# Cutting sixteen weight rows into transfers of 5, 5, 5 and 1 instead of four of 4

## The chip, the core and the metric

The kernel runs on one core of one Trainium2 chip. The metric is the device time of one execution in microseconds. A core has five engines with instruction streams of their own: PE (matrix multiply), DVE (vector), ACT (scalar), POOL and SP. SP does no arithmetic here; it issues the transfers from the chip's main memory into the core's working memory, which has 128 rows ("partitions"). The transfers themselves are carried by 16 DMA engines.

## The reference

Two identical rounds, each an attention block over a long cache for one new token and then a gated feed-forward block, in float32, for two sequences:

```python
B, Sq, D = 2, 1, 512
Hq, Hkv, Sk, Dh = 32, 8, 32768, 128
...
q = (x @ wq).reshape(B, Sq, Hq, Dh).transpose(0, 2, 1, 3)
k = jnp.repeat(k_cache, Hq // Hkv, axis=1)
v = jnp.repeat(v_cache, Hq // Hkv, axis=1)
p = softmax(einsum("bhqd,bhkd->bhqk", q, k) * Dh ** -0.5)
o = einsum("bhqk,bhkd->bhqd", p, v)
A(x) = o.transpose(0, 2, 1, 3).reshape(B, Sq, Hq * Dh) @ wo
B(x) = (gelu(x @ w_gate) * (x @ w_up)) @ w_down        # 512 -> 1792 -> 512
...
x = x + A(layernorm(x)); x = x + B(layernorm(x))
x = x + A(layernorm(x)); x = x + B(layernorm(x))
```

The two caches are read in full in both rounds: over a gigabyte of float32 in all, for little arithmetic on each byte.

## The kernel before

The work is a stream. All inputs are listed once, at the start, in the order in which they will be used (`add`, lines 246 to 275): for each of the two layers the query weights, then for each of the 16 pairs of a cache head and a sequence its keys and values, with the output weights of a head between the halves of its values, and last the feed-forward weights. Layer 1 walks the pairs backwards, so that it begins with what layer 0 has still in memory.

One large tile, `mem`, of 110 units of 512 float32 in each of 128 partitions, takes everything. A full cache piece is 32 units: 64 KB in each of 128 partitions, 8.4 MB. `pump` (line 193) takes the next entry of the stream, looks for a free place in `mem`, and issues its transfer on the SP queue; when there is no place it stops, and is called again whenever `done` gives a place back. So three cache pieces circulate, and SP issues a transfer as soon as the matmuls that read the old content have ended. Transfers of one queue are carried in the order of their issue.

For each pair, `scores` multiplies the keys (L443), `softmax` follows on DVE and ACT, `values` multiplies the values (L512), and `combine` and `project` multiply the result by the head's output weights into the accumulator W.

Nearly all transfers fill 128 partitions. For two heads, listed in `NARROW`, a part of the output weights is laid out otherwise: 2 of 4 query heads' weights of cache head 6 in layer 0, and 3 of 4 of cache head 1 in layer 1. They lie in 16 partitions (`NROW`) as 8 groups (`NSEL`) per query head. A row holds 8 x 512 float32 for each query head: 32 KB in layer 0, 48 KB in layer 1. `narrow` (line 532) uses them: it spreads the result over 16 rows (L538) and multiplies group by group (L546). The remaining query heads' weights come by an ordinary 128-partition transfer issued right behind, and are used in L556.

The sixteen rows are fetched by four transfers, number i taking rows i, i + 4, i + 8 and i + 12. The host arranges `won` so that these four lie together. All four go out one after another on the SP queue (L209) as soon as there is room, and `narrow` waits for all of them.

Of the kernel before, what the change touches and what calls it, by code (L numbers as in the profile page):

```python
# [18 lines left out]
HKV = 8  # L19
REP = 4  # L20
DM = 512
# [42 lines left out]

NARROW = {(0, HKV - 2): 2, (1, 1): 3}
NROW = 16
NSEL = P // NROW


def pieces(split):  # L70

    out, s = [], 0
    for n in split:
        out.append((s, n))
        s += n
    return out


def parts(kind, l, pair):

    if kind == "k":
        return K_PARTS[l].get(pair, pieces(PLAIN))
    return pieces(V_SPLIT[l].get(pair, PLAIN))
# [59 lines left out]
def block_kernel(ctx: ExitStack, tc: tile.TileContext, x, consts, kt, vt, wq, wo, won, gu, wd, out):  # L143
    nc = tc.nc
# [5 lines left out]
    mem = cp.tile([P, UNITS * UNIT], F32, name="mem")  # L150
# [6 lines left out]
    def take(key, n):  # L157
        if key in planned:
            o = planned[key]
            if not any(s <= o and o + n <= e for s, e in holes):  # L160
                return None
        elif n == CHUNK:
            spots = [o for o in range(0, UNITS - CHUNK + 1, CHUNK)
                     if any(s <= o and o + n <= e for s, e in holes)]
            if not spots:
                return None
            o = spots[0]
        else:
            fit = [(e - s, -s, e) for s, e in holes if e - s >= n]
            if not fit:  # L170
                return None
            size, s, e = min(fit)
            o = -s
        for i, (s, e) in enumerate(holes):
            if s <= o and o + n <= e:
                holes[i:i + 1] = [(x, y) for x, y in ((s, o), (o + n, e)) if y > x]
                return o
        return None
# [14 lines left out]
    def pump():  # L193
        while stream:
            key, src, rows, cols = stream[0]
            n = CHUNK if rows == NROW else cols / UNIT if key in planned else -(-cols // UNIT)
            o = take(key, n)
            if o is None:
                return
            stream.popleft()  # L200
            if key == LAST_ROOM:
                held.append(ROOM[1])
            c = int(o * UNIT)
            at[key] = (o, n), mem[:rows, c:c + cols]
            if rows == NROW:


                for i in range(4):
                    nc.sync.dma_start(mem[i:NROW:4, c:c + cols], src[i])  # L209
            else:  # L210
                nc.sync.dma_start(at[key][1], src)

    def flat_of(key):
        if key not in at:
            pump()
        return at[key][1]

    def get(key, a):
        return flat_of(key).rearrange("p (a c) -> p a c", a=int(a))

    def done(key, s=0, n=None):

        o, size = at[key][0]
        n = size if n is None else n
        if s + n == size:
            del at[key]
        give(o + s, n)
        pump()
# [3 lines left out]
    def flat(src, g, b, s, n):  # L232
        h, c = divmod(s, CHUNK)
        return src[b, g, h, :, c * UNIT:(c + n) * UNIT]

    def add(key, src, rows, cols):
        stream.append((key, src, rows, cols))

    def meets(l, n):

        return (l == 0 and n == len(ORDER) - 1), (l == 1 and n == 0)

    def wo_group(l, g):
        return next(t for t in WO_GROUPS[l] if g in t)

    for l in range(2):
        for i, (s, m) in enumerate(pieces(WQ_SPLIT[l])):
            add(("wq", l, i), wq[:, s * DM:(s + m) * DM], P, m * DM)
        for n, (g, b) in enumerate(orders[l]):
            second = meets(l, n)[1]  # L250
            vp = parts("v", l, (g, b))
            for s, m in parts("k", l, (g, b)):
                add(("k", l, g, b, s), flat(kt, g, b, s, m), P, m * UNIT)
            for s, m in [] if second else vp:
                if n % 2 == 1 and s == vp[1][0] and not meets(l, n)[0]:
                    group = wo_group(l, g)
                    o = g % 2 * HALF
                    if (l, g) in NARROW:
                        h = NARROW[l, g]
                        add(("won", l, g), won[l, :, :, :h * NSEL * DM], NROW, h * NSEL * DM)  # L260
                        add(("wo", l, g), wo[g // 2, :, o + h * DM:o + HALF], P, (REP - h) * DM)
                    elif len(group) == 2 and g == group[0]:
                        add(("wo", l, g), wo[g // 2], P, 2 * HALF)
                    elif len(group) == 1:
                        add(("wo", l, g), wo[g // 2, :, o:o + HALF], P, HALF)
                add(("v", l, g, b, s), flat(vt, g, b, s, m), P, m * UNIT)
            if meets(l, n)[0]:

                add(("wo", l, g), wo[g // 2, :, g % 2 * HALF:(g % 2 + 1) * HALF], P, HALF)
        for e in range(2):  # L270
            half_of = gu[e * P * FH:(e + 1) * P * FH].rearrange("(p c) -> p c", p=P)
            for j, (c, m) in enumerate(pieces(GU_SPLIT[l][e])):
                add(("gu", l, KC * e + j), half_of[:, c:c + m], P, m)
        for j, (o, m) in enumerate(pieces(WD_SPLIT[l])):
            add(("wd", l, j), wd[:, o * DM:(o + m) * DM], P, m * DM)
# [15 lines left out]
    nc.scalar.dma_start(xT, x)  # L291
    nc.scalar.dma_start(cst, consts)
    pump()
    ident = cst[:, C_ID:C_ID + P]

# [44 lines left out]
    def big():  # L340

        state["turn"] = 1 - state["turn"]
        if state["alone"] or state["turn"]:
            return big_desk[:, :]
        return mem[:, held[0] * UNIT:(held[0] + 1) * UNIT]
# [186 lines left out]
    def narrow(l, g, oT, final):  # L532
# [3 lines left out]
        n = heads * NB  # L536
        for j in range(NSEL):
            nc.tensor.matmul(m[:NROW, n * j:n * j + n], ident[:, NROW * j:NROW * j + NROW],  # L538
                             oT[:, :heads, :].rearrange("p t b -> p (t b)"), start=True, stop=True)
        on = big()[:NROW, :NSEL * n]  # L540
        nc.vector.tensor_copy(on, m[:NROW, :NSEL * n])
        w = get(("won", l, g), NSEL * heads)
        for i in range(NSEL * heads):
            q = i % 4
# [234 lines left out]
```

## Time and profile before

| | |
|---|---|
| median of 3 runs | 2569.77 us (2569.65 to 2570.94) |
| the profiled execution | 2569.96 us |
| its span, first to last instruction | 2568.2 us |
| matmul busy | 1321.7 us, 51% of the span |
| vector, scalar busy | 142.6 us, 81.5 us |
| read from main memory | 1103.18 MB, 430 GB/s over the span |
| share of the 16 DMA engines' time | 99.6% for the SP queue |

A transfer shows in the profile as packets. Here a packet is one row of one transfer on one DMA engine, and each DMA engine that has a part in a transfer ends it with a packet of 4 bytes that reports its part as landed. So the count of packets under 512 B in a short window says how many engines reported in it. A transfer has landed when all its reports are in. "L209" is line 209 of the kernel; "SPq" is an issue on SP's queue; "in_won" is the narrow output weights, "in_wo" the wide ones, "in_kt" and "in_vt" the caches, "in_gu" and "in_wd" the feed-forward weights. The chain of waits is followed back from the last instruction, at each step to what released it.

### The profile page before, as it was taken

The numbers are of one execution on the slowest core, as the hardware profiler recorded it, in microseconds if no ns is written. First come the engines' busy times: TensorE is split into PE (matmuls) and PEld (weight loads), VectorE is DVE, ScalarE is ACT, GpSimd is POOL, SyncE is SP. The second block draws the span as 40 slices with busy tenths as digits, with TensorE's granted clock in tenths as the row PEclk, the third lists the DMA queues.
The fourth block names the chain that finished last, engine by engine and source line by source line (L and its number), as shares of the span: only waits on it lengthen the run. The fifth ranks groups of instructions, "written<-read, shape, count | busy, mean of one in ns | idle before, by whom it ended". The sixth has DMA issues, their size and how long they took to land.

```text
span 2568.2 us, 19786 instructions
## 1 busy us (share of the span) xinstructions
PE 1321.7 (51%) x9266; PEld 333.2 (13%) x9266; DVE 142.6 (6%) x483; ACT 81.5 (3%) x188; POOL 2.4 (0%) x8
## 2 busy tenths in 40 slices
PE   3544454445544554464686554454445444554656
PEld 1111111111111111111121111111111111111112
DVE  0000000000000000000011000000000000000001
ACT  0000000000000000000000000000000000000000
POOL 0000000000000000000000000000000000000000
PEclk8777777777777777777798777777776777777778
DMA  9999999999999999999999999999999999999998
GB/s 425 426 437 429 432 435 432 433 433 431 433 432 431 437 427 437 431 432 429 427 409 437 431 433 433 433 433 434 430 435 430 433 432 435 428 437 430 431 431 372
DMA packets 26929, 1104.51 MB, mean 430 GB/s; under 512 B 3136, under 2 KB 3392, under 8 KB 6080
## 3 DMA queue, kind: packets, MB, share of 16 engines
q1 hardware_dynamic: 26560, 1103.18, 99.6%
q8 instruction: 72, 1.18, 0.2%
q10 hardware_dynamic: 288, 0.08, 0.0%
q14 instruction: 9, 0.07, 0.0%
HBM read 1103.18 MB, written 0.07 MB: 430 GB/s over the span
## 4 chain that ended last, share of the span: by engine, by line
DMA 69%; PE 22%; another core or an unknown queue 7%; DVE 1%; ACT 1%; issue 0%; SPq 0%; POOL 0%; ACTq 0%; DVEq 0%
DMA mem<-in_vt 48%; DMA mem<-in_kt 16%; PE A L512 12%; PE S L443 8%; DMA mem<-in_gu 2%; DMA aux<-in_consts 2%; DMA mem<-in_wq 1%; PE W L546 0%; PE W L564 0%; PE M L525 0%; DMA mem<-in_wd 0%; ACT big L521 0%; PE W L586 0%; PE A L443 0%
## 5 line engine op out<-in xcount | busy, mean ns | idle before, releaser
L443 PE MATMUL S<-mem,aux 128*32 128x512 f32 x4032 | 578.5, 737 | 527.8 <-DMA mem<-in_kt 527.3
L512 PE MATMUL A<-mem 128*16 128x512 f32 x2048 | 292.7, 735 | 256.6 <-DMA mem<-in_vt 256.6
L512 PE MATMUL A<-mem,big 128*16 128x512 f32 x2048 | 288.0, 725 | 259.3 <-DMA mem<-in_vt 259.3
L443 PEld LDWEIGHTS S<-mem,aux 128*32 128x32 f32 x4032 | 145.8, 133 | 948.1 <-issue 511.7
L512 PEld LDWEIGHTS A<-mem 128*16 128x16 f32 x2048 | 61.6, 113 | 473.0 <-DMA mem<-in_vt 273.3
L512 PEld LDWEIGHTS A<-mem,big 128*16 128x16 f32 x2048 | 61.1, 112 | 471.1 <-DMA mem<-in_vt 276.3
L446 DVE TENSOR_REDUCE aux<-S 128x1 f32<-128x512 f32 x63 | 43.6, 692 | 1114.3 <-PE S L443 1114.3
L486 ACT ACTIVATE T<-S,aux 128x512 f32<-128x512 f32 x63 | 41.4, 657 | 1194.1 <-DVE aux L482 1194.1
L530 DVE TENSOR_REDUCE aux<-M 128x4 f32<-128x64 f32 x32 | 7.2, 226 | 1133.6 <-PE M L525 1133.6
L492 PE MATMUL M<-aux 128*128 128x4 f32 x64 | 15.2, 307 | 88.3 <-DVE aux L490 88.3
L521 ACT ACTIVATE mem<-A,aux 128x512 f32<-128x512 f32 (+1 forms) x17 | 11.1, 662 | 582.9 <-PE A L512 582.9
L521 ACT ACTIVATE big<-A,aux 128x512 f32<-128x512 f32 (+1 forms) x17 | 11.2, 662 | 562.7 <-PE A L512 562.7
L478 PE MATMUL M<-aux 128*128 128x128 f32 x32 | 10.3, 323 | 34.5 <-DVE aux L476 34.5
L492 PEld LDWEIGHTS M<-aux 128*128 128x128 f32 x64 | 12.3, 241 | 94.4 <-DVE aux L490 94.4
L488 DVE STREAM_TRANSPOSE big<-T 128x512 f32<-128x512 f32 x32 | 22.9, 717 | 14.5 <-ACT T L486 14.5
L488 DVE STREAM_TRANSPOSE mem<-T 128x512 f32<-128x512 f32 x32 | 23.0, 718 | 13.5 <-ACT T L486 13.5
L402 PE MATMUL M<-mem,aux 128*32 128x512 f32 x128 | 20.4, 684 | 4.3 <-DMA mem<-in_wq 3.9
L525 PE MATMUL M<-aux,mem 128*128 128x128 f32 x64 | 10.6, 287 | 12.4 <-ACT mem L521 12.4
L525 PE MATMUL M<-aux,big 128*128 128x128 f32 x64 | 10.6, 287 | 12.4 <-ACT big L521 12.4
L564 PE MATMUL W<-mem,aux 128*2 128x512 f32 x96 | 12.5, 592 | 3.8 <-DVE aux L530 3.8
L362 PE MATMUL A<-aux 128*128 128x256 f32 (+2 forms) x42 | 14.3, 421 | 0.3 <-DVE aux L379 0.3
L478 PEld LDWEIGHTS M<-aux 128*128 128x128 f32 x32 | 4.3, 133 | 63.5 <-DVE aux L476 63.5
(122 smaller groups left out, 214.2 us busy)
## 6 DMA issues: line engine op xcount, KB each, us to landing
mem<-in_wo SPq DMA_DIRECT2D x5, 2048.0 KB, 53.6
mem<-in_gu SPq DMA_DIRECT2D x10, 896.0 KB, 8.0
mem<-in_vt SPq DMA_DIRECT2D x2, 4096.0 KB, 42.5
mem<-in_kt SPq DMA_DIRECT2D x1, 7168.0 KB
mem<-in_kt SPq DMA_DIRECT2D x6, 1024.0 KB, 8.2
mem<-in_vt SPq DMA_DIRECT2D x3, 2048.0 KB, 43.7
mem<-in_wq SPq DMA_DIRECT2D x6, 1024.0 KB, 8.2
mem<-in_kt SPq DMA_DIRECT2D x1, 6144.0 KB
```

The costliest lines, as they stand in the source:

```text
L362: nc.tensor.matmul(bank, ident[:, :bank.shape[0]], part.to_broadcast([P, n]), start=True, stop=True)
L402: nc.tensor.matmul(qp[32 * t:32 * t + 32, :], window(k, v), w[:, i - s, :], start=(i < 4), stop=(i >= 8 * KC - 4))
L443: nc.tensor.matmul(banks[u][32 * t:32 * t + 32, :], pad[:, PAD_Q - 4 * c:PAD_Q + 32 - 4 * c], w[:, j - s, :], start=(j == tile_of[0]), sto ...
L446: nc.vector.tensor_reduce(mx[:, u:u + 1], banks[u], axis=AX.X, op=OP.max)
L478: nc.tensor.transpose(m[:, :P], nm.to_broadcast([P, P]), ident)
L486: nc.scalar.activation(T[u], banks[u], AF.Exp, bias=bias, scale=SCALE, accum_out=ls[:, u:u + 1])
L488: nc.vector.transpose(p[u], T[u])
L492: nc.tensor.matmul(m[:, :REP], both.to_broadcast([P, P]), same, start=True, stop=True)
L512: nc.tensor.matmul(A[32 * t:32 * t + 16, :], p[u][:, at_p:at_p + 16], w[:, QUAD * i + t, :], start=(j == 0), stop=(j == NU // QUAD - 1))
L521: nc.scalar.activation(md[:, i:i + 512 // n], A[:, i:i + 512 // n], AF.Copy, scale=linv)
L525: nc.tensor.transpose(m[:, c * P:(c + 1) * P], md[:, c * P:(c + 1) * P], ident)
L564: nc.tensor.matmul(W[32 * t:32 * t + NB, :], oT[:, t, :], w[:, o + t, :], start=first, stop=final)
```

## The change

The sixteen rows come by four transfers of 5, 5, 5 and 1 rows. The first three take every third row out of the first fifteen, beginning with row 0, 1 and 2; the fourth takes row 15. The host keeps `won` in the order of its rows, since the transfers now pick theirs. Each row lands where it landed before.

```diff
 NROW = 16
+NROW_CUTS = [slice(0, 15, 3), slice(1, 15, 3), slice(2, 15, 3), slice(15, 16)]
...
-                for i in range(4):
-                    nc.sync.dma_start(mem[i:NROW:4, c:c + cols], src[i])
+                for r in NROW_CUTS:
+                    nc.sync.dma_start(mem[r, c:c + cols], src[r])
...
-                        add(("won", l, g), won[l, :, :, :h * NSEL * DM], NROW, h * NSEL * DM)
+                        add(("won", l, g), won[l, :, :h * NSEL * DM], NROW, h * NSEL * DM)
...
-        "won": f(np.asarray(A_wo).reshape(HKV, REP, NSEL, 4, 4, DM)[[g for _, g in NARROW]]
-                 .transpose(0, 4, 3, 1, 2, 5)).reshape(len(NARROW), 4, 4, REP * NSEL * DM),
+        "won": f(np.asarray(A_wo).reshape(HKV, REP, NSEL, NROW, DM)[[g for _, g in NARROW]]
+                 .transpose(0, 3, 1, 2, 4)).reshape(len(NARROW), NROW, REP * NSEL * DM),
```

## The prediction

> **What bounds the kernel now.** I read the page first, its line on DMA packets, its queues and the shares of its chain of waits:
>
> ```profile
> DMA packets 26929, 1104.51 MB, mean 430 GB/s; under 512 B 3136, under 2 KB 3392, under 8 KB 6080
> ...
> q1 hardware_dynamic: 26560, 1103.18, 99.6%
> q8 instruction: 72, 1.18, 0.2%
> ...
> DMA 69%; PE 22%; another core or an unknown queue 7%; DVE 1%; ACT 1%; issue 0%; SPq 0%; POOL 0%; ACTq 0%; DVEq 0%
> ```
>
> The sixteen DMA engines are busy for 99.6% of the span with the SP queue alone, and nearly every link of the chain is a cache transfer or the matmuls that wait for one. A change that moves no byte more or less can therefore act only by who carries the bytes. So the next view is the packets of short windows. The first row below is 1000 to 1019.4 us, the second 1101 to 1109.7 us:
>
> ```profile
> DMA packets 144, 8.39 MB, mean 432 GB/s; under 512 B 16, under 2 KB 16, under 8 KB 16
> DMA packets 235, 3.87 MB, mean 444 GB/s; under 512 B 48, under 2 KB 48, under 8 KB 176
> ```
>
> The first is one cache transfer's worth: 8.39 MB in 128 rows of 64 KB, and sixteen packets under 512 B. Each engine ends its share with one small report. Sixteen engines carry eight rows each in 19.4 us, so a 64-KB row costs 2.42 us on its engine, which is 27.1 GB/s, and in proportion a 32-KB row (the narrow ones of layer 0) 1.21 and a 48-KB row (layer 1) 1.82. The second window holds the ends of a cache transfer, of the four narrow transfers and of the wide one behind them: 48 reports = 16 + 16 + 16, so four narrow transfers report sixteen times, four each. Four rows go to four engines, one row each.
>
> The reports also show how far the engines are apart. The rows below are the 128-row transfers that end just before and just behind the narrow weights. Layer 0: 1081.8 to 1084.2, 1086.5 to 1088.3, then 1121.8 to 1122.8, 1126.5 to 1129. Layer 1: 2331.5 to 2334.4, 2337.4 to 2338.5, then 2371.2 to 2372.2, 2376.8 to 2379, 2380.9 to 2381.
>
> ```profile
> DMA packets 24, 1.05 MB, mean 437 GB/s; under 512 B 8, under 2 KB 8, under 8 KB 8
> DMA packets 23, 0.98 MB, mean 546 GB/s; under 512 B 8, under 2 KB 8, under 8 KB 8
> DMA packets 10, 0.39 MB, mean 393 GB/s; under 512 B 4, under 2 KB 4, under 8 KB 4
> DMA packets 30, 1.18 MB, mean 472 GB/s; under 512 B 12, under 2 KB 12, under 8 KB 12
> DMA packets 27, 1.25 MB, mean 429 GB/s; under 512 B 8, under 2 KB 8, under 8 KB 8
> DMA packets 17, 0.59 MB, mean 536 GB/s; under 512 B 8, under 2 KB 8, under 8 KB 8
> DMA packets 14, 0.66 MB, mean 655 GB/s; under 512 B 4, under 2 KB 4, under 8 KB 4
> DMA packets 27, 1.05 MB, mean 477 GB/s; under 512 B 11, under 2 KB 11, under 8 KB 11
> DMA packets 4, 0.20 MB, mean 1966 GB/s; under 512 B 1, under 2 KB 1, under 8 KB 1
> ```
>
> Ahead of the narrow weights eight engines report early and eight some five microseconds later; behind them four are early and twelve late. So the four carriers come out of the early eight: four rows of 1.21 us (4.85) carry them back among the late ones, and in layer 1 four rows of 1.82 us (7.28) carry one of them 9.7 us behind the first, alone, while the other eleven are in by 2379.
>
> What this lag is worth shows where a layer ends. The fence holds layer 0, windows 1238 to 1238.9, 1244 to 1244.5, 1245 to 1245.4 and 1245.7 to 1246; then layer 1, 2469.6 to 2470.5, 2473.9 to 2475.7 and 2477.6 to 2477.8; then engines and DMA share by the microsecond, and the chain:
>
> ```profile
> DMA packets 12, 0.49 MB, mean 546 GB/s; under 512 B 4, under 2 KB 4, under 8 KB 4
> DMA packets 14, 0.46 MB, mean 918 GB/s; under 512 B 7, under 2 KB 7, under 8 KB 7
> DMA packets 5, 0.26 MB, mean 655 GB/s; under 512 B 1, under 2 KB 1, under 8 KB 1
> DMA packets 2, 0.07 MB, mean 218 GB/s; under 512 B 1, under 2 KB 1, under 8 KB 1
> DMA packets 15, 0.72 MB, mean 801 GB/s; under 512 B 4, under 2 KB 4, under 8 KB 4
> DMA packets 27, 1.05 MB, mean 583 GB/s; under 512 B 11, under 2 KB 11, under 8 KB 11
> DMA packets 4, 0.20 MB, mean 983 GB/s; under 512 B 1, under 2 KB 1, under 8 KB 1
> 2557.00:2558.00 1.00, 0.64 (x5) 0.09 (x1) 0.20 (x1) 0.47 (x1) 0.00 (x0) 1.00 0.77 307
> 2562.00:2563.00 1.00, 1.00 (x6) 0.24 (x10) 0.00 (x0) 0.60 (x1) 0.00 (x0) 1.00 0.17 66
> 2563.00:2564.00 1.00, 1.00 (x40) 0.97 (x44) 0.00 (x0) 0.00 (x0) 0.00 (x0) 1.00 0.06 25
> 2564.00:2565.00 1.00, 1.00 (x40) 0.60 (x31) 0.00 (x0) 0.00 (x0) 0.00 (x0) 1.00 0.02 8
> 2519.42 36.70 DMA mem<-in_gu
> 2556.16 1.11 PE A L665 x2
> ```
>
> A share of 0.77 is twelve of sixteen engines, 0.06 is one. From 2557 us four engines have nothing left, and from before 2563 to about 2564.3 a single engine works alone. The last compute chain (2556.16) starts on the arrival of the gate and up weights, queued in front of this, so I take it that the same engine brought them last. The kernel is bound by its latest engine, not by the sixteen together: a microsecond off the latest shortens the end, one off any other does nothing.
>
> **The change, part by part.**
>
> *Issues and the wait for the weights: nothing.* Here are the SP queue, the issue times and the use in both layers:
>
> ```profile
> 1075.74 2.63 SPq L209 DMA_DIRECT2D mem<-in_won  x4
> 1078.41 0.44 SPq L211 DMA_DIRECT2D mem<-in_wo  x1
> 1097.36 0.33 SPq L211 DMA_DIRECT2D mem<-in_vt  x1
> 1140.72 4.84 PE W L546 x32
> 2393.11 7.93 PE W L546 x48
> ```
>
> Four issues stay four (2.63 us for all), with the wide issue and then 18 us of nothing on SP behind them; a tenth more would be hidden, and if that cover were gone it would cost 0.3 us. The narrow weights have landed by 1109.7 and are used at 1140.72, 31 us of margin, so even ten microseconds later in landing stalls no matmul. What lies in memory is the same, row for row, so the matmuls of L546 are as before.
>
> *Relief of the old four.* Five rows on five engines three times is three rows for each of five engines, and one row more. The old four lose a row each: 1.21 us in layer 0, 1.82 in layer 1. In layer 0 the latest engine (about 7.7 us behind the first at 1246) had its last slip behind 1129, where nobody was later than 7.2: it has slipped since, and I take it for one of the late eight, so the relief is worth 0 there. In layer 1 the latest is the one alone, 8.1 us behind the first at 2477.7 with the next not beyond 6.1; taking 1.82 off it leaves 6.2, a gain of 1.6 when rounded to what the next allows. Sum: **-1.6 us**, and 0 at worst.
>
> *The sixteenth row.* A transfer of one row isn't in the trace. It lies between one engine for the whole row (1.21 and 1.82 us, which gives one of the old four its fourth row back and may eat the whole 1.6) and sixteen engines for a sixteenth each (0.08 and 0.11 us). I take the second for the sum because it changes least, and the first for the range.
>
> The Trainium skill ("DMA: Bandwidth & Descriptors", section on why a DMA increments its semaphore by 16) says that the engine count is the largest number up to 16 that divides the slowest dimension, and that the lowest-numbered ones are taken. The 48 reports agree for four rows; by it a bare row would go to one engine, one of the old four, and the relief would fall from 1.6 to between 1.6 and 0 us, which no run so far shows.
>
> *The fifth engine.* It gets three rows, 3.64 us and 5.46 us, that it did not have. Which side it stands on no row says. Among the early ones (the four that stay early report within 1.0 us in both layers) it comes to 1.0 + 3.64 = 4.6 us in layer 0, under the 7.7 of the latest, and to 1.0 + 5.46 = 6.5 in layer 1, level with the relieved latest: 0. This cover gone, it is the other side: among the late eight it becomes the latest, 6.3 (the seven reports of 1244 to 1244.5) + 3.64 - 7.7 = +2.2 in layer 0, and from the middle of the eleven reports of 2473.9 to 2475.7, 5.4 + 5.46 - 8.1 = +2.8 in layer 1, **+5.0**.
>
> *Whose rows they are.* The old cut takes rows four apart, i, i+4, i+8, i+12, so over its four transfers an engine writes one aligned block of four neighbouring rows, and no other engine writes into that block. The new cut takes rows three apart: engine 0 writes rows 0 to 2, engine 1 writes 3 to 5, engine 2 writes 6 to 8, engine 3 writes 9 to 11, engine 4 writes 12 to 14. Blocks are now crossed: row 3 belongs to engine 0's old block, 6 and 7 to engine 1's, 9 to 11 to engine 2's, 12 to 14 to engine 3's. If memory takes each block at one engine's rate, and if the owner streams other rows there as it did before, crossing costs both. No row of the trace shows two engines in one block. Below: nothing. Above: both run at half speed while they meet. The nearest row for that is the instruction queue, the only other stream that shares something with q1: 0.2% of sixteen engines over 2568.2 us for 72 packets is about 1.1 us for 16 KB, where 27.1 KB per us would give 0.6, so sharing a path does halve.
>
> The upper bound for engine 3, the worst placed: three rows of its own at half speed (six row times) and three of engine 4's into its block (three more) are nine row times where it had four, +5: 6.07 and 9.10 us. Were it also the latest carrier (7.1 us at 1245.4 in layer 0, 8.1 in layer 1): 7.1 + 6.07 - 7.7 = +5.4, and +9.1, together +14.5. The five come to their rows 0 to 2.9 us apart, while three rows take 3.6 to 5.5: for about half of the time the neighbour is away from its block as well and nothing is lost. I take the middle between -1.6 and +14.5: **+6.4 us**.
>
> The Trainium skill ("SBUF — State Buffer", section on the DMA port swizzle) groups partitions 0-3, 4-7, 8-11 and 12-15 as four ports, each shared by its four. That rule speaks against this change: by it the crossing costs the upper bound for as long as two engines meet, and the sum would lie between 6.4 and 14.5, where a memory without such ports would leave -1.6. No run so far shows which.
>
> *Sum.* The profiled execution took 2569.96 us around a span of 2568.2, 0.19 above the median 2569.77. 2569.96 + 6.4 = 2576.4, and in terms of the median 2576.2.
>
> **The rivals.**
>
> *Early and unshared (faster by a hair).* The fifth engine is early and blocks don't matter: -1.6, 2568.2 in terms of the median. For it: no row shows sharing, and eight engines are early with only four taken. Against it: nothing in the trace has yet tried crossing blocks. This is also what a change that does nothing looks like (2569.8).
>
> *Late and unshared.* +5.0, 2574.8. It decides from the point where the fifth engine reports with the late eight ahead of the narrow weights; four early and eight late are left for it, and nothing ties a number to a side.
>
> *Late and shared.* The fifth engine writes its three rows into a block that engine 3, five microseconds ahead, streams into by then, so here the meeting is nearly full: six row times. 6.3 + 7.28 - 7.7 = +5.8 and 5.4 + 10.92 - 8.1 = +8.2, together +14.0, 2583.8. For it: lag and sharing add up without cover. Against: needs both.
>
> **How the numbers follow.** Early and shared, the forecast: 0.42, and by itself 2570 to 2580. Late and shared: 0.27. Early and unshared: 0.15. Late and unshared: 0.14. Something else: 0.02. I give sharing 0.69 because the one place where two streams meet in this trace shows halving, and the early side a little more than half because the old four all came from it. About 0.2% (5.1 us) is what a measurement of this kernel can tell from no change. Slower by more than that: of the forecast 0.6, of late and shared nearly all, of late and unshared half: 0.25 + 0.27 + 0.07 = 0.59, with the rest of the unnamed 0.61. Same: 0.16 + 0.14 + 0.07 = 0.37, less a little, 0.36. Faster by that much needs more than the relief can give: 0.03. The range holds the early unshared case at its foot and the late shared one at its top: 2568.0 to 2585.0.
>
> **What would show it.** Four narrow issues of about 2.6 us at the same place. The reports behind the narrow weights: five engines moved instead of four, so three early and thirteen late, if the fifth was early; still four early, and one far behind all, if it was late. With sharing, the packets' share of time rises above what the bytes explain, and the latest report behind the weights in layer 1 is beyond 9.7 us; without it, it falls to about 7.9 us behind the first. The stretch with one engine alone at the end grows with sharing and shrinks without. If the matmuls of L546 wait, or the SP queue stalls on L209, the whole working by lag is wrong; so it is if the time moves while the distance of the latest report doesn't.

## The result and the profile after

The changed kernel takes 2578.3 us in the median of seven runs (2576.36 to 2579.61), the kernel before 2569.75 in the same setting. The ratio is 1.0033, with a 95% interval of 1.002 to 1.0045: **slower by 8.5 us**. One of the seven executions of the kernel before took 2926.34 us and is left out of the ratio. The profiled execution took 2578.3 us around a span of 2576.5, 8.3 more than before.

The page of the changed kernel hardly differs:

```profile
DMA packets 26929, 1104.51 MB, mean 429 GB/s; under 512 B 3136, under 2 KB 3392, under 8 KB 6080
...
q1 hardware_dynamic: 26560, 1103.18, 99.6%
q8 instruction: 72, 1.18, 0.2%
...
DMA 71%; PE 21%; another core or an unknown queue 7%; DVE 0%; ACT 0%; issue 0%; SPq 0%; POOL 0%; ACTq 0%; DVEq 0%
```

The count of reports, 3136, is that of before. Four transfers of four rows reported sixteen times; 5 + 5 + 5 + 1 do so too. So five rows go to five engines, one row each, and the single row goes to one engine.

The time is lost at two places. These are links of the chain of waits (start, length, what), first of the kernel before, then of the changed one:

```profile
1097.36 32.02 DMA mem<-in_vt
1129.42 8.74 PE A L512 x64
...
2348.80 32.63 DMA mem<-in_vt
```

```profile
1098.22 34.40 DMA mem<-in_vt
1132.67 9.72 PE A L513 x64
...
1144.95 3.85 PE W L547 x32
...
1386.05 48.70 DMA mem<-in_vt
...
2351.09 38.68 DMA mem<-in_vt
...
2401.61 7.79 PE W L547 x48
...
2564.50 1.11 PE A L666 x2
```

The cache transfer queued around the narrow weights makes the matmuls wait 34.4 us where it was 32.0 in layer 0, and 38.7 where it was 32.6 in layer 1: +2.4 and +6.1. The last compute chain starts 8.3 us later (2564.50 against 2556.16). The matmuls of the narrow weights (L546, now L547) wait for nothing new.

What happens at these places is best seen in bytes. The rows are 1096 to 1112 us and 2348 to 2372 us, of before, then of the changed kernel. The last two columns are the DMA engines' busy share and GB/s:

```profile
1096.00:1112.00 16.00, 5.85 (x35) 1.39 (x31) 3.04 (x11) 1.45 (x4) 0.00 (x0) 0.69 1.01 431
2348.00:2372.00 24.00, 11.61 (x75) 2.66 (x67) 3.04 (x11) 1.45 (x4) 0.00 (x0) 0.71 1.00 431
```

```profile
1096.00:1112.00 16.00, 4.44 (x33) 1.31 (x27) 3.04 (x11) 1.45 (x4) 0.00 (x0) 0.64 1.02 356
2348.00:2372.00 24.00, 9.84 (x75) 2.43 (x67) 3.04 (x11) 1.45 (x4) 0.00 (x0) 0.72 1.00 347
```

The engines are as busy as before and move a sixth to a fifth less. By an estimate from these rows, what is missing is worth 16 x (431 - 356) / 431 = 2.8 us in layer 0 and 24 x (431 - 347) / 431 = 4.7 in layer 1. A busy share says nothing about speed here: 1.01 goes with 431 GB/s and 1.02 with 356, since a packet that takes longer counts as busy for longer.

The reports behind the narrow weights, of the changed kernel: layer 0, 1124.1 to 1124.5, 1128.7 to 1130.9 and 1132.1 to 1132.2; layer 1, 2377.8 to 2378.5, 2383.3 to 2385.5, 2386.7 to 2386.8 and 2389.2 to 2389.4:

```profile
DMA packets 9, 0.39 MB, mean 983 GB/s; under 512 B 3, under 2 KB 3, under 8 KB 3
DMA packets 28, 1.05 MB, mean 477 GB/s; under 512 B 12, under 2 KB 12, under 8 KB 12
DMA packets 2, 0.07 MB, mean 655 GB/s; under 512 B 1, under 2 KB 1, under 8 KB 1
DMA packets 8, 0.33 MB, mean 468 GB/s; under 512 B 3, under 2 KB 3, under 8 KB 3
DMA packets 26, 0.98 MB, mean 447 GB/s; under 512 B 11, under 2 KB 11, under 8 KB 11
DMA packets 2, 0.07 MB, mean 655 GB/s; under 512 B 1, under 2 KB 1, under 8 KB 1
DMA packets 2, 0.07 MB, mean 328 GB/s; under 512 B 1, under 2 KB 1, under 8 KB 1
```

Three engines are early where four were: the fifth carrier came out of the early ones. But those three, which carry no narrow row, report from 1124.1 on, where the first four reported from 1121.8 on, and from 2377.8 against 2371.2. (Of the 6.6 us in layer 1, 2.4 were there ahead of the narrow weights already: the first reports there come at 2333.9 against 2331.5.) Whatever slows the carriers slows engines that have no part in it. The latest in layer 1 is 11.4 us behind the first, 9.7 before, and at the end one engine works alone for longer:

```profile
2570.00:2571.00 1.00, 1.00 (x6) 0.30 (x2) 0.00 (x0) 0.60 (x1) 0.00 (x0) 1.00 0.07 29
2571.00:2572.00 1.00, 1.00 (x29) 0.71 (x32) 0.00 (x0) 0.00 (x0) 0.00 (x0) 1.00 0.06 25
2572.00:2573.00 1.00, 1.00 (x44) 0.77 (x36) 0.00 (x0) 0.00 (x0) 0.00 (x0) 1.00 0.04 16
```

From 2570 to beyond 2572 about one of sixteen engines is busy (0.07, 0.06, 0.04); in the kernel before there are two such rows, 0.06 and 0.02.

### The profile page after: what moved, and what is told of

Its sections match the earlier page's. It is cut to its first block, busy times and chain, and to the rows that moved or that the text cites. A ratio compares the mean times of both kernels' runs of the same rounds, so it can differ in the third digit from the quotient of the medians.

```text
span 2576.5 us, 19786 instructions
## 1 busy us (share of the span) xinstructions
PE 1307.3 (51%) x9266; PEld 330.2 (13%) x9266; DVE 142.5 (6%) x483; ACT 81.4 (3%) x188; POOL 2.4 (0%) x8
## 2 busy tenths in 40 slices
DMA packets 26929, 1104.51 MB, mean 429 GB/s; under 512 B 3136, under 2 KB 3392, under 8 KB 6080
## 3 DMA queue, kind: packets, MB, share of 16 engines
q1 hardware_dynamic: 26560, 1103.18, 99.6%
## 4 chain that ended last, share of the span: by engine, by line
DMA 71%; PE 21%; another core or an unknown queue 7%; DVE 0%; ACT 0%; issue 0%; SPq 0%; POOL 0%; ACTq 0%; DVEq 0%
DMA mem<-in_vt 49%; DMA mem<-in_kt 17%; PE A L513 12%; PE S L444 7%; DMA mem<-in_gu 2%; DMA aux<-in_consts 2%; DMA mem<-in_wq 1%; PE W L547 0%; DMA mem<-in_wd 0%; PE M L526 0%; PE W L565 0%; ACT big L522 0%; PE W L587 0%; PE A L444 0%
## 5 line engine op out<-in xcount | busy, mean ns | idle before, releaser
L444 PE MATMUL S<-mem,aux 128*32 128x512 f32 x4032 | 569.5, 727 | 537.2 <-DMA mem<-in_kt 536.7
```

Source lines behind the costliest of these rows:

```text
L444: nc.tensor.matmul(banks[u][32 * t:32 * t + 32, :], pad[:, PAD_Q - 4 * c:PAD_Q + 32 - 4 * c], w[:, j - s, :], start=(j == tile_of[0]), sto ...
```

## The experiments

Three theories stood. *Crossed blocks*: two engines that write into one aligned block of four rows slow each other. *Fifth engine*: five engines, or a number that is no power of two, is what hurts. *Source*: the rows of a transfer lie farther apart in main memory. A row is called crossed below when its engine writes it into a block that another engine fills. Where no other kernel is named, the diffs are against the changed one. They are shortened: what follows from the lines shown, in the loop around the transfers, in the host's order and in the matmuls, is left out.

**The old cut from the new order in main memory.**

```diff
-NROW_CUTS = [slice(0, 15, 3), slice(1, 15, 3), slice(2, 15, 3), slice(15, 16)]
+NROW_CUTS = [slice(i, 16, 4) for i in range(4)]
```

> The old cut (rows i, i+4, i+8, i+12) from the new order in main memory, where the four rows of a transfer lie 256 KB apart instead of 64 KB. Theory 'crossed blocks' (two DMA engines writing into one aligned block of four rows slow each other and the rest): nothing is crossed, so the time of the kernel before, 2569.8 us within 1 us, and all 32-KB packets at 1.21 us. Rival 'source' (the rows' distance in main memory slows the reads): at least as slow as the changed kernel, 2576 to 2580. Rival 'fifth engine' (five engines, or a count that is no power of two, is what hurts): 2569.8, as for the first theory.

Measured 2570.7 us against 2569.91, ratio 1.0004 (0.9994 to 1.0013). The source is not it: the rows of a transfer lie four rows apart in main memory here, in the changed kernel three, and the two windows (1096 to 1112 and 2348 to 2372 us) run at 443 and 429 GB/s.

**The new cut from the old order in main memory.** The converse:

```diff
+NROW_FROM = [slice(0, 5), slice(5, 10), slice(10, 15), slice(15, 16)]
+NROW_ORDER = [*range(0, 15, 3), *range(1, 15, 3), *range(2, 15, 3), 15]   # the host's order of rows
...
-                    nc.sync.dma_start(mem[r, c:c + cols], src[r])
+                    nc.sync.dma_start(mem[r, c:c + cols], src[f])
```

> The changed kernel's cut of 5, 5, 5 and 1 rows, but main memory holds the rows of each transfer next to each other, as for the kernel before (64 KB apart). 'Crossed blocks' and 'fifth engine': as slow as the changed kernel, 2576 to 2580. 'Source': back at 2568 to 2570.

Measured 2577.74 against 2569.91, 1.0028 (1.0017 to 1.004): as slow as the change. "Source" has fallen on both sides.

**Five engines, each in its own block** (against the kernel before; the host adds four rows of zeros):

```diff
-                    nc.sync.dma_start(mem[i:NROW:4, c:c + cols], src[i])
+                    nc.sync.dma_start(mem[i:NROW + 4:4, c:c + cols], src[i])
```

> Four transfers of five rows, i, i+4, i+8, i+12, i+16: sixteen rows as before and four rows of zeros into partitions 16 to 19, which nobody uses; 320 KB more in all. Five engines, each in its own block. 'Crossed blocks': no packet is stretched; the fifth engine is one of the early ones and takes four rows (4.85 and 7.28 us) behind its cover, so 2569 to 2571. 'Fifth engine': slowed like the changed kernel, 2576 to 2580, since five engines carry rows here too, and one row more than there.

Measured 2570.13 against 2569.91, 1.0001 (0.9992 to 1.0011). The reports behind the weights, 1121.4 to 1122 and 1126.3 to 1129:

```profile
DMA packets 10, 0.46 MB, mean 765 GB/s; under 512 B 3, under 2 KB 3, under 8 KB 3
DMA packets 35, 1.44 MB, mean 534 GB/s; under 512 B 13, under 2 KB 13, under 8 KB 13
```

Three early and thirteen late, as in the changed kernel, but at the old times. The fifth engine is an early one, and its four rows cost nothing that can be measured. "Fifth engine" has fallen.

**Four engines, crossed.**

```diff
-NROW_CUTS = [slice(0, 15, 3), slice(1, 15, 3), slice(2, 15, 3), slice(15, 16)]
+NROW_CUTS = [slice(0, 12, 3), slice(1, 12, 3), slice(2, 12, 3), slice(12, 16)]
```

> Transfers of rows 0,3,6,9 / 1,4,7,10 / 2,5,8,11 / 12,13,14,15: four engines and four rows each as before, but three engines write into blocks that another of the four owns. 'Crossed blocks': stretched packets on all engines again, slower than before by 4 to 9 us, 2574 to 2579. 'Fifth engine' and 'the engine's row count': 2569.8, since engines and bytes for each are those of the kernel before. 'Source': between, as the rows are 192 KB apart in three of the four transfers.

Measured 2577.9 against 2569.91, 1.0032 (1.0019 to 1.0044). Engines, rows for each and bytes are those of the kernel before; only the blocks are crossed, and that alone brings 8.0 us. (Nine rows are crossed, and all four engines write some of them, in their order: 12 / 3, 13 / 6, 7, 14 / 9, 10, 11.)

The loss is made up otherwise than in the changed kernel, though. These are the two windows, and then the reports behind the narrow weights of layer 1, 2373.8 to 2374.7, 2378.7 to 2384.3 and 2387 to 2387.7:

```profile
1096.00:1112.00 16.00, 5.79 (x39) 1.45 (x35) 3.04 (x11) 1.45 (x4) 0.00 (x0) 0.73 1.02 398
2348.00:2372.00 24.00, 12.67 (x91) 3.01 (x83) 3.04 (x11) 1.45 (x4) 0.00 (x0) 0.72 1.00 399
```

```profile
DMA packets 11, 0.46 MB, mean 510 GB/s; under 512 B 4, under 2 KB 4, under 8 KB 4
DMA packets 49, 2.56 MB, mean 456 GB/s; under 512 B 10, under 2 KB 10, under 8 KB 10
DMA packets 8, 0.39 MB, mean 562 GB/s; under 512 B 2, under 2 KB 2, under 8 KB 2
```

The rate of all engines falls less: it is worth 1.2 + 1.8 = 3.0 us, where the profiled execution, with a span of 2574.8 us, is 6.6 longer. The rest shows as lag: the latest report comes at 2387.6, 13.7 us behind the first, where it was 9.7 before and 11.4 with the change.

**The changed transfers, uncrossed.**

```diff
+NROW_TO = [slice(0, 20, 4), slice(1, 20, 4), slice(2, 20, 4), slice(3, 4)]
...
-                    nc.sync.dma_start(mem[r, c:c + cols], src[r])
+                    nc.sync.dma_start(mem[to, c:c + cols], src[r])
```

> The changed kernel's transfers, 5, 5, 5 and 1 rows with the same rows of main memory, but they go to partitions 0, 4, 8, 12, 16 / 1, 5, ... / 2, 6, ... / 3, so each of the five engines keeps to its own block. The matmuls still read partitions 0 to 15, so the part of the result that these weights give is left out as such; the work in time is the same. 'Crossed blocks': no packet stretched, nothing of the 8.5 us is left: 2568 to 2570, the relief of the old four less what the sixteenth row gives back. 'The count of rows or engines matters too': between 2571 and 2578.

Measured 2568.56 against 2569.89, 0.9994 (0.9985 to 1.0003): nothing of the 8.5 us is left. This is the change without the crossing. Its -1.3 us is the relief of the old four less what the sixteenth row gives back; the interval, -3.9 to +0.8 us, does not tell it from none.

**All four engines in one block.**

```diff
-NROW_CUTS = [slice(0, 15, 3), slice(1, 15, 3), slice(2, 15, 3), slice(15, 16)]
+NROW_CUTS = [slice(4 * i, 4 * i + 4) for i in range(4)]
```

> Four transfers of four neighbouring rows, 4i to 4i+3: four engines as before, but in each transfer all four write into one block, and twelve of the sixteen rows lie in a block of another engine. 'Crossed blocks': four engines share one block's rate, so rows take up to four times 1.21 us; slower than the changed kernel, 2580 to 2590. 'Only the number of engines counts': 2569.8.

Measured 2586.14 against 2569.85, 1.0062 (1.0048 to 1.0076): +16.3. With twelve rows crossed, and four engines in one block at a time, it is about twice as dear as the changed cut.

**The old cut at partitions 64 to 79, and at 32 to 47** (against the kernel before; the matmuls read the rows there):

```diff
+BASE = 64                      # 32 in the other kernel
-                    nc.sync.dma_start(mem[i:NROW:4, c:c + cols], src[i])
+                    nc.sync.dma_start(mem[BASE + i:BASE + NROW:4, c:c + cols], src[i])
```

> The old cut, but the sixteen rows lie in partitions 64 to 79 instead of 0 to 15, and the matmuls read them there. The four carriers keep out of each other's block, but all four write into blocks that four other engines fill in the 128-row transfers. 'A block belongs to one engine's stream, whoever else comes is in the way': all sixteen rows are crossed, slower by at least as much as the change, 2576 to 2586. 'Only carriers that meet each other in one block matter': 2569.8.

> The old cut into partitions 32 to 47, read there. If partitions 32 higher belong to the same way into memory as those 32 lower, the four carriers stay at home: 2569.8, no packet stretched. If the ways follow the plain order of partitions, the rows lie in the blocks of other engines, and it is as slow as with partitions 64 to 79: 2585 to 2590.

At 64: 2587.29 against 2569.85, 1.0069 (1.0054 to 1.0085). At 32: 2569.74 against 2569.89, 0.9999 (0.999 to 1.0008). The window 1096 to 1112 us, first at 64, then at 32:

```profile
1096.00:1112.00 16.00, 2.49 (x23) 0.68 (x15) 3.04 (x11) 1.45 (x4) 0.00 (x0) 0.72 0.96 262
```

```profile
1096.00:1112.00 16.00, 5.70 (x35) 1.38 (x31) 3.04 (x11) 1.45 (x4) 0.00 (x0) 0.68 1.02 435
```

At 64 each carrier keeps to a block that no other carrier writes, and yet the rate falls to 262 GB/s. At 32 nothing happens. So it is not the block of four partitions as such that counts. Both results fit ways into memory that partitions 0 to 15 and 32 to 47 share and 64 to 79 do not, and of which each engine fills one of its own in the 128-row transfers; at 64 the carriers are then in the way of other engines' cache rows.

**Eight engines, each in its own block** (against the kernel before): the narrow weights in 32 rows, half as long, by four transfers of eight.

```diff
-NROW = 16
+NROW = 32
```

> The narrow weights in 32 rows instead of 16, each half as long, by four transfers of eight rows (i, i+4, ..., i+28): eight engines, each in its own block, half the bytes for each. Theory (only the latest engine counts; eight engines are early; no blocks crossed): if all eight carriers are early ones, layer 0 is as before (latest not a carrier) and layer 1 loses its lone late carrier, 8.1 us behind the first before, 6.4 now: 2568.2, -1.6 us. If some of engines 5 to 7 are late ones: 6.3 + 2.4 - 7.7 and 5.4 + 3.6 - 8.1, together +2 us. Rival (any transfer that isn't 128 rows slows all engines, by its number of engines): slower than 2576.

Measured 2573.92 against 2569.85, 1.0016 (1.0007 to 1.0025). Windows 1096 to 1112, and the reports in 1121.4 to 1122.3, 1123.9 to 1126.1, 1126.25 to 1128 and 1130.2 to 1130.8:

```profile
1096.00:1112.00 16.00, 5.73 (x35) 1.36 (x31) 3.04 (x11) 1.45 (x4) 0.00 (x0) 0.68 1.02 435
```

```profile
DMA packets 10, 0.52 MB, mean 583 GB/s; under 512 B 2, under 2 KB 2, under 8 KB 2
DMA packets 20, 0.92 MB, mean 417 GB/s; under 512 B 6, under 2 KB 6, under 8 KB 6
DMA packets 20, 0.92 MB, mean 524 GB/s; under 512 B 6, under 2 KB 6, under 8 KB 6
DMA packets 6, 0.26 MB, mean 437 GB/s; under 512 B 2, under 2 KB 2, under 8 KB 2
```

The rate is the old one, as it should be with nothing crossed. But two early engines are left over, and two reports come beyond 1130.2, 2 us behind the rest: six of the eight carriers were early and two late ones. Two late engines with 64 KB more in layer 0 and 96 KB in layer 1 make the whole kernel 4.1 us slower, where I had put 2 on that case. Here the lag sets the time, without any crossing.

**Eight engines and more weights laid out so** (against the 32-row version):

```diff
-NARROW = {(0, HKV - 2): 2, (1, 1): 3}
+NARROW = {(0, HKV - 2): 3, (1, HKV - 2): 3, (1, 1): 3}
```

> As the 32-row version, with more weights laid out so: three heads instead of two in layer 0, and in layer 1 three more, of cache head 6. Each head moved takes 16 KB (0.6 us) off the late eight and puts 0.6 us more on the eight carriers. Theory: 0.6 us less in layer 0 and 1.8 less in layer 1 than the 32-row version, 2565.8. Rival (the place that the extra narrow weights hold in memory stalls the stream): no gain, or slower than 2570.

Measured 2576.06 against 2569.85, 1.0024 (1.0015 to 1.0033). That is 2.1 us slower even than the 32-row version. The gain that I expected hung on eight early carriers, which that version does not have. The rival has something for it as well: from 1280 to 1300 us the DMA engines are busy for 0.88 of the time, in the 32-row version for 0.94 and in the kernel before for 0.97, so the engines run dry for longer there. Why they do was not shown.

**Two narrow heads in layer 1** (against the kernel before):

```diff
-NARROW = {(0, HKV - 2): 2, (1, 1): 3}
+NARROW = {(0, HKV - 2): 2, (1, 1): 2}
```

> The kernel before with two narrow heads instead of three in layer 1: each carrier has 64 KB less (2.4 us), every engine 16 KB more (0.6). Theory 'only the latest engine counts': the lone carrier at 8.1 us behind the first falls to about 6.3, the others rise with all by 0.6, so layer 1 ends about 1.2 us earlier: 2568.6. Rival 'the sum over the engines counts': no change, 2569.8.

Measured 2569.74 against 2569.89, 0.9998 (0.9989 to 1.0006). Inconclusive: the interval, -2.8 to +1.5 us, holds the expected -1.2 and no change alike. None of these versions beats the kernel before by more than a measurement can tell.

**One row crossed** (against the kernel before):

```diff
+                nc.sync.dma_start(mem[24:25, c:c + cols], src[0, 0:1])
```

> The kernel before with a fifth narrow transfer of a single row (a copy of row 0) into partition 24, which nobody reads: one row more on the first engine, written into the block of the seventh engine, which streams its cache rows there. What is open is why the crossing slows all sixteen engines. 'Only the pair shares': about 2 to 4 stretched packets in each layer, 2.4 and 3.6 us of stretch in all. 'A crowded block holds up the others too': stretched packets on most engines, several times that. For the time: the first engine has 1.21 and 1.82 us more and meets for as long again; if it is the latest in layer 1, up to 2573.5, if it is not, 2570 to 2571.

Measured 2571.55 against 2569.83, 1.0006 (0.9997 to 1.0016): +1.7, not clear of noise. The packets tell more. I added up by how much those of the two windows, 1096 to 1112 and 2348 to 2372 us, take longer than their bytes would at 27.1 GB/s, and took off the same sum for the kernel before (2.3 and 1.9). With one row crossed this stretch is 3.4 and 4.8 us, somewhat above the 2.4 and 3.6 of a pair that shares. The changed kernel has 47 and 73 us, over all sixteen engines. Nine of its rows lie in a block of another engine, ten if the last one is carried by the first engine; at two row times each that gives at most 24 and 36. So ten crossed rows cost twice the sum of ten pairs here, and hit engines that have no part. That is not a rule by the number of rows: with four engines crossed the stretch is 23 and 28 us, where nine pairs give 22 and 33. Why one cut spreads and the other hardly does is open.

## Why the prediction was right, and where it was off

*Bound by the latest engine:* half right. The time does follow the latest report behind the narrow weights of layer 1: it moves from 2380.9 to 2389.3 with the change (+8.4; the span +8.3), and to 2387.6 with four engines crossed (+6.7; the span +6.6). The 32-row version shows lag alone, without a loss of rate. The signs named for sharing came too: 11.4 us instead of 9.7 in layer 1, and a longer stretch with one engine alone. The busy share did not rise, though; it stayed at 99.6% while the rate fell. And what makes the latest engine late was mostly something else than its own rows. The forecast's own test against the working by lag, "if the time moves while the distance of the latest report doesn't", nearly came true in layer 0: the first reports move from 1121.8 to 1124.1 while the latest is 8.0 us behind them, 7.2 at most before. In the changed kernel most of the loss is not lag of one engine but rate of all: 2.8 + 4.7 = 7.5 us by the two windows, and the lone stretch at the end about one more.

*Issues and the wait for the weights:* right. Four issues take 2.75 and 2.60 us, and nothing waits on them:

```profile
1074.91 2.75 SPq L210 DMA_DIRECT2D mem<-in_won  x4
2329.49 2.60 SPq L210 DMA_DIRECT2D mem<-in_won  x4
```

*The fifth engine:* right, early (three early, thirteen late) and free. Both "late" rivals, with 0.41, fall with that.

*The sixteenth row:* I took sixteen engines for the sum; it is one. The reports show it: 3136 with the change, the same as before, and two more, 3138, with the extra single-row transfers. The rule that I cited from the Trainium skill ("DMA: Bandwidth & Descriptors", the section on why a DMA increments its semaphore by 16) agrees with the four, five and eight reports of transfers of four, five and eight rows. For a bare row I read too much into it: it counts the slowest dimension that is not of size 1, and says that software can split a bare row, so that one engine is what the runs show and not what the Trainium skill says.

*Relief of the old four:* By its own rows it is 1.82 us in layer 1; the 1.6 is what the fifth engine, put at 6.5 of 8.1, would leave of it. Relief and sixteenth row together measured -1.3 us uncrossed, forecast -1.6; the measured figure cannot be told from none.

*Whose rows they are:* the mechanism was right, and it is the whole of the change. "Early and unshared" fell; the uncrossed kernel is what it described, at 2568.56 where it said 2568.2. The size was short: the crossing was put at 8.0 us (from -1.6 to +6.4) and is 9.9 (from -1.3 to +8.5). The step that failed is the one that charged the crossing to engine 3 alone, halved for the time in which neighbours miss each other. The runs show a loss of rate on all engines in its place, 431 to 356 and 347 GB/s, and the 6.4 was only the middle between two bounds, so that it came near is partly luck. The ground for half speed, the instruction queue, is tied to blocks of rows by no row of the trace; the nearest to a test is the one crossed row, whose stretch is 1.3 to 1.4 times that of a pair at half speed. The port rule of the Trainium skill ("SBUF — State Buffer", DMA port swizzle) is borne out by the runs, its pairing of partitions 32 apart too (-0.2 us at 32, +17.4 at 64).

## What to carry to other kernels

Where a transfer has fewer rows than partitions, ask of each row two things: which DMA engine carries it, and which way into memory it enters by. With every engine on the way that it fills in the large transfers, the rate stayed what it was in all the cuts tried here (429 to 452 GB/s in the two windows); the bytes still cost time where they fall on a late engine (4.1 us in the 32-row version). The same sixteen rows cut across cost 8.5 us, where the better balance had about one to give. And look at GB/s beside the busy share: a share of 1.02 with 356 GB/s means packets that take longer, not more bytes.

## What I had not expected of the hardware

A few crowded ways can pull down the rate of all sixteen engines: 431 to 356 and 347 GB/s in the changed kernel, to 398 and 399 with nine rows crossed by four engines, to 262 in layer 0 with sixteen rows at partitions 64 to 79. Engines without any of these rows reported 2.3 us later in layer 0 of the changed kernel. And the engines are not alike in lag: of the eight that carry the 32-row version's narrow weights, two are late ones, so that 64 KB more on two of sixteen engines in layer 0 and 96 KB in layer 1 go with 4.1 us in the time of the whole kernel.
